# Moving the last rows' scores ahead of both value parts in an attention and mixture-of-experts kernel

## The chip, the cores and the metric

The kernel runs on one core of a Trainium2 chip. The time is device time in microseconds of one execution. The core has five engines, each with its own instruction stream: TensorE (PE; its weight loads are PEld), VectorE (DVE), ScalarE (ACT), GpSimd (POOL) and SyncE (SP, which issues most transfers).

## The reference

Three layers follow each other; the change lies in the first.

```python
# 1. attention: 4 batches, 8 heads, 576 positions, 64 columns per head
scores = scale * q @ k.T                       # per batch and head
cum = cumsum(maximum(s, 0)); bias = -(cum[:, None] - cum[None, :])
scores = where(causal, -1e9, scores + minimum(bias, 0))
attn = exp(scores - max(scores)); attn = attn / (sum(attn) + 1e-9)
x = (attn @ v) as (2304 tokens, 512)
# 2. mixture of experts: every token goes to the expert of its largest logit
logits = x @ w_gate; e = argmax(logits); gate = softmax(logits)[e]
x[tokens of e] = gate * (maximum(x[tokens of e] @ w1[e], 0) @ w2[e])    # 8 experts, 512 -> 1024 -> 512
# 3. three products and a maximum
h = maximum(maximum(x @ u1, x @ u2), x @ u3)                             # 512 -> 768
out = h @ w_out                                                          # 768 -> 512
```

## The kernel before, in words

The 32 heads are worked off as 16 pairs, and each pair p is spread over three periods. In period p its scores are formed and turned into exponentials; in period p+1 the exponentials are transposed and multiplied with the values; in period p+2 the result (oT) is turned back to rows, scaled by the sums and stored (`xrow`). So a period of the middle holds the scores of one pair, the transposes and value parts of the pair before, and the rows of the one before that. After the last period the expert layers follow, TensorE's matmuls nearly alone.

Every step is a Python function that is put into a heap with a place (`at(slot, fn)`), and at the end the functions are called in order of place (`run_events`). The order of calls is the order of instructions on each engine; the engines then run freely and wait for each other's data and buffers. A place is counted in slots of 0.456 us (`SLOT`) and a period is 25 slots (`IT`). The table `SEQ` (L93) gives the places of TensorE's steps in a period in microseconds; the steps that follow on other engines stand a number of slots later: `LR` (2.5) from scores to their reduction, `LE` (5.5) to the exponential, `LH` (1.5) from a transpose to its copy, `LV` (1.0) from a value part to its copy, `LN` (3.5) from the tail's exponential to its normalisation.

The steps of a period, by their names in `SEQ`:

- `s0` to `s7` are scores of the first 512 rows of both heads, in blocks of 128 rows (`scores`, L290): row block 3 (s0, s1, 512 columns), 1 (s2, s3), 2 (s4, s5, 384 columns) and 0 (s6, s7). TensorE writes two banks at s0, s2, s4 and s6 (L308). VectorE adds the bias and takes the minimum (`red`, L314) into one of three `ns` buffers, and ScalarE takes the exponential with its sum (`ex`, L321).
- `s8` and `s9` are the last rows, or the tail: the 64 rows from 512 of both heads in one block of 128, columns 0 to 255 and 256 to 575 (`tmm`, L328). Their reductions (`tred`, L335) write one buffer `nst`, one exponential follows (`tex`, L343), and `tnorm` divides by the sum (two small VectorE instructions, L348 and L349, and one of GpSimd, L350).
- `A0`, `B0`, `A1`, `B1`, `C2`, `C3` and `TT` are transposes of exponentials (`t_mm`, L376) into two banks in turn, copied into one buffer `ptT` (`t_ev`, L409): A1, B1 and TT by VectorE (L414), the others by ScalarE (L416). TT holds the tail's columns 0 to 511; its copy writes four strips of 64 columns per head, at 512, 960, 1408 and 1856 of `ptT`.
- `v0` and `v1` are the value parts (`v_mm`, L418): v0 makes output columns 0 to 255, from columns 0 to 255 and 576 to 703 of `ptT`, and v1 columns 256 to 575, from all key blocks and with the tail's strips in them. Each writes one of two banks that `xrow` uses too. `v_ev` (L430, L435) copies them to `oT`; at v0's copy GpSimd also clears the last columns of `oT`.
- `x0` and `x1` are the rows of the pair before the last (L459, L464).

Score banks ("a") are four, taken in turn; the tail takes one bank each for s8 and s9. The last pair has its own order (`LSEQ`, `lpos`). When a batch of heads is finished, `route` (L475) puts some thirty small VectorE instructions and two groups of small matmuls, at steps of 1.8 or 1.6 slots, into the next periods. Three expert weights are split in two parts during the attention, by ScalarE (`w_hi`, L192) and VectorE (`w_lo`, L685), at slots 80, 126 and 172.

Of the kernel before, what the change touches and what calls it, by code (L numbers as in the profile page):

```python
# [59 lines left out]
T0, T1, T2, T3, T4 = -56, -56, -53, -51, -43  # L60
F0, F1, F2, F3 = 7, 9, 11, 19
BCE = "VAVAA"
LR, LE, LH, LV, LX, LN = 2.5, 5.5, 1.5, 1.0, 1.5, 3.5
NSB, PPB = 3, 4
CSL = 22
MA, MB, MT = 8, 0.5, 0
# [24 lines left out]


SEQ = {"A0": 0, "B0": 0.45, "s0": 0.9, "s1": 0.9, "s2": 1.95, "s3": 1.95, "A1": 2.65, "B1": 3.0, "x0": 3.35, "x1": 4.15,  # L93
       "s4": 4.7, "s5": 4.7, "s6": 5.55, "s7": 5.55, "C2": 6.0, "C3": 6.45, "v0": 6.8, "TT": 7.65, "s8": 8.1, "s9": 8.55,
       "v1": 9.1}
TDVE = ("A1", "B1", "TT")

# [1 line left out]
def emit(nc, tc, qt, kt, v, s, wg, w1, w2, m64, out, dbg=None):  # L99
# [9 lines left out]
    def bank(tag, dt=F32):  # L109
        return ps.tile([P, 512], dt, tag=tag, name="ps_" + tag, bufs={"a": 4, "b": 2, "c": 2}[tag])  # L110
# [49 lines left out]
    for b in (0, B - 1):  # L160
        t = cp.tile([P, 5, NG], F32, name=f"gx{b}")
# [26 lines left out]
    NP = B * H // 2  # L188
# [13 lines left out]
    def at(slot, fn, *args):  # L202
        heapq.heappush(evq, (slot, next(seqno), fn, args))
# [61 lines left out]
    def masks(p, t0, t1, t2):  # L265

        def wide():
            t = st[p]["bl"][:, 0:2048].rearrange("p (x w) -> p x w", w=512)[:, :, 128:256]
            G.affine_select(t, t, pattern=[[0, 4], [-1, 128]], compare_op=ALU.is_ge, fill=BIG, base=0,
                            channel_multiplier=1)  # L270

        def narrow(g):
            t = st[p]["bl"][:, 1024 * g:1024 * g + 768].rearrange("p (x w) -> p x w", w=128)[:, 0:5:4]
            G.affine_select(t, t, pattern=[[0, 2], [-1, 128]], compare_op=ALU.is_ge, fill=BIG, base=0,
                            channel_multiplier=1)

        def tail():
            for g in range(2):
                t = st[p]["bl"][64 * g:64 * g + 64, BW - 64:BW]
                G.affine_select(t, t, pattern=[[-1, 64]], compare_op=ALU.is_ge, fill=BIG, base=0, channel_multiplier=1)  # L280

        at(t0, wide)
        for g in range(2):
            at(t1[g], narrow, g)
        at(t2, tail)
# [84 lines left out]
    def ptv(p, tslots, vslots):  # L370
        d = st[p]

        def tr(pt, c, i, g, k0):
            T.transpose(pt[:, c:c + 128], (d["P", "t"] if g == "t" else d["P", g, i])[:, k0:k0 + 128], idf)  # L374

        def t_mm(u):  # L376
            pt = d["pt", u] = bank("b")
            if u[0] in "AB":
                g, j = "AB".index(u[0]), int(u[1])
                for i in range(j, 4):  # L380
                    tr(pt, 128 * (i - j), i, g, 128 * j)
            elif u == "C2":
                for g in range(2):
                    for i in (2, 3):
                        tr(pt, 256 * g + 128 * (i - 2), i, g, 256)
            elif u == "C3":
                for g in range(2):
                    tr(pt, 128 * g, 3, g, 384)
                tr(pt, 256, 0, "t", 512)
            else:  # L390
                for j in range(4):
                    tr(pt, 128 * j, 0, "t", 128 * j)

        def regions(u):
            pt = d["pt", u]
            two = lambda ap: ap.rearrange("p (g w) -> p g w", g=2)
            if u[0] in "AB":
                g, j = "AB".index(u[0]), int(u[1])
                w = 512 - 128 * j
                return [(lambda t: t[:, g, POFF[j]:POFF[j] + w], pt[:, :w])]  # L400
            if u == "C2":
                return [(lambda t: t[:, :, POFF[2]:POFF[2] + 256], two(pt))]
            if u == "C3":
                return [(lambda t: t[:, :, POFF[3]:POFF[3] + 128], two(pt[:, 0:256])),
                        (lambda t: t[:, :, POFF[4]:POFF[4] + 64], two(pt[:, 256:384]))]
            return [(lambda t: t[:, :, 512:PTW].rearrange("p g (j w) -> p g j w", w=64)[:, :, 0::TS // 64],
                     pt.rearrange("p (j g w) -> p g j w", j=4, g=2))]

        def t_ev(u):  # L409
            if "pt" not in st[p]:  # L410
                d["pt"] = ab.tile([P, 2, PTW], F32, tag="ptT", name="ptT", bufs=1)
            for f, src in regions(u):
                if u in TDVE:
                    V.tensor_copy(f(d["pt"]), src)  # L414
                else:
                    A.activation(f(d["pt"]), src, AF.Copy)  # L416

        def v_mm(x):  # L418

            c0, c1 = ((0, 256), (256, 576))[x]  # L420
            po = d["po", x] = bank("c")
            js = [j for j in range(5) if 128 * j < c1]
            for j in js:
                qa = max(c0, 128 * j)
                for g in range(2):
                    T.matmul(po[64 * g:64 * g + 64, qa - c0:c1 - c0], d["v"][:, g, j],  # L426
                             d["pt"][:, g, POFF[j] + qa - 128 * j:POFF[j] + c1 - 128 * j],
                             start=(j == 0), stop=(j == js[-1]))

        def v_ev(x):  # L430
            c0, c1 = ((0, 256), (256, 576))[x]
            if x == 0:
                d["oT"] = ab.tile([P, 640], F32, tag="oT", name="oT", bufs=2)
                G.memset(d["oT"][:, S:640], 0.0)
            A.activation(d["oT"][:, c0:c1], d["po", x][:, :c1 - c0], AF.Copy)  # L435

        for u, t in tslots.items():
            at(t, t_mm, u)
            at(t + LH, t_ev, u)
        for x, t in vslots.items():  # L440
            at(t, v_mm, x)
            at(t + LV, v_ev, x)

    def xrow(p, slots):
        d = st[p]
# [140 lines left out]
    for p in range(NP):  # L586
        t = IT * p
        load(p, t - 2 * IT + LD0 if p else -60)

        last_wide = [max(t + pos[f"s{2 * ORD.index(i) + g}"] for i in (1, 3)) + LR for g in range(2)]  # L590
        first = [min(t + pos[f"s{2 * ORD.index(i) + g}"] for i in (0, 2)) for g in range(2)]
        masks(p, t - 4 if p == 0 else t + min(pos[f"s{x}"] for x in range(4)) - MA,
              [max(last_wide[g] + 0.1, first[g] - MB) for g in range(2)], t - MT)
        scores(p, [t + pos[f"s{i}"] for i in range(10)])
        o = t + IT
        units = ("A0", "A1", "B0", "B1", "C2", "C3", "TT")
        tpos = {u: o + pos[u] for u in units}
        vpos = {x: o + pos[f"v{x}"] for x in range(2)}
        xpos = [o + IT + pos["x0"], o + IT + pos["x1"]]
        lpos = {u: IT * NP + LS0 + LSP * i for i, u in enumerate(LSEQ.split())}  # L600
        if p == NP - 2:
            xpos = [lpos["y0"], lpos["y1"]]
        if p == NP - 1:
            tpos = {u: lpos[u] for u in units}
            vpos = {x: lpos[f"v{x}"] for x in range(2)}
            xpos = [lpos["x0"], lpos["x1"]]
            for x in range(2):
                vpos[x] = max([vpos[x]] + [tpos[u] + LH + 0.02 for u in units if x or u[0] in "AB"])
            xpos[0] = max(xpos[0], max(vpos.values()) + LV + 0.02)
            xpos[1] = max(xpos[1], xpos[0] + 0.5)  # L610
        ptv(p, tpos, vpos)
        end = xrow(p, xpos)
        if p == NP - 1 - H // 2:
            TR2 = end
# [30 lines left out]
    t = TE  # L645
    S0, SL = [], []
    for x, gs in enumerate(STEPS):
        if x == NEARLY:
            t = TM
# [6 lines left out]
    def pt(g, i):  # L656

        x, k = step[g]
        us = SL[x] / 8 * i + sum(cost[o] for o in STEPS[x][:k]) / 8 + (GAP12 if i >= 4 else 0)
        return S0[x] + us / SLOT  # L660
# [99 lines left out]
    for n in range(24):  # L760
        dst = w32 if n < 18 else wo32
        i, x = divmod(n if n < 18 else n - 18, 2)
# [233 lines left out]
    for x, gs in enumerate(STEPS):  # L996
# [7 lines left out]
        for g in gs:  # L1004
# [8 lines left out]
            for kk in range(4):  # L1013
                t = t0 + st_ * kk
# [5 lines left out]
            for f in range(8):  # L1020
                t = pt(g, f // 2) + (f % 2) * L / 16 / SLOT
# [5 lines left out]
            for d_ in range(4):  # L1027
                t = pt(g, 4 + d_)
# [210 lines left out]
```

## Time and profile before

| | us |
|---|---|
| median of 3 runs | 795.99 (795.22 to 797.65) |
| profiled execution | 794.54 |
| its span, from first to last instruction | 792.8 |
| PE busy | 758.3 (96%) |
| PEld busy | 681.6 (86%) |
| DVE busy | 437.1 (55%) |
| ACT busy | 335.2 (42%) |
| POOL busy | 109.4 (14%) |

The busy times are sums over all instructions of an engine, and the shares are averages over a stage of attention (to about 200 us) and the expert stages behind it. A timeline row gives the start in us, the duration, the engine, the line, the operation, what it writes and reads, and the count; in brackets stands the idle time of the engine before it and who ended it. A matmul of 32-bit data appears as several instructions.

### The profile page before, as it was taken

The page shows a single profiled execution, that of the slowest core. Times are in us where ns is not written, and L with a number is a line of the kernel's source. Part 1 is how long each engine was busy: PE and PEld are TensorE (multiplying, and loading weights), DVE is VectorE, ACT ScalarE, POOL GpSimd, SP SyncE. Part 2 cuts the span into 40 slices and gives each one's busy share as a digit, 9 for nine tenths or more (in the row PEclk, how much of TensorE's full clock was granted, in tenths as well). Part 3 has the DMA queues.
Part 4 walks back from the last instruction along what each step waited for, and adds up shares of the span by engine and source line. Part 5 has one row for each costly group of instructions (what it writes and reads, how often), then busy time and mean ns, then how long its engine had stood idle before and what let it go on. Part 6 is the DMA issues. An engine that isn't in the chain of part 4 may idle for free. (4 is left out here: it accounts for less than half of the span.)

```text
span 792.8 us, 12891 instructions
## 1 busy us (share of the span) xinstructions
PE 758.3 (96%) x4782; PEld 681.6 (86%) x4782; DVE 437.1 (55%) x1142; ACT 335.2 (42%) x771; POOL 109.4 (14%) x226
## 2 busy tenths in 40 slices
PE   6999899999889999999999999999999999999996
PEld 4666666666789998999999999989999899898995
DVE  5667757678668686899888756412312223122120
ACT  5666666666546343555455544221121212212111
POOL 3332332333030200101200000010010000100001
PEclk9999999999999999999999999999999999999999
DMA  5887858767386687868776535000010000100001
GB/s 154 238 216 217 212 160 225 194 181 222 135 281 210 221 310 256 308 221 281 238 230 214 204 97 172 26 31 10 1 41 1 26 14 1 41 1 14 26 1 41
DMA packets 34876, 112.43 MB, mean 142 GB/s; under 512 B 4793, under 2 KB 4875, under 8 KB 32891
## 3 DMA queue, kind: packets, MB, share of 16 engines
q1 hardware_dynamic: 24107, 81.66, 34.6%
q10 hardware_dynamic: 7456, 18.89, 6.7%
q0 software_dynamic: 3248, 11.03, 4.1%
q8 instruction: 39, 0.64, 0.3%
q14 instruction: 26, 0.21, 0.1%
HBM read 94.97 MB, written 16.60 MB: 141 GB/s over the span
## 5 line engine op out<-in xcount | busy, mean ns | idle before, releaser
L1135 DVE TENSOR_TENSOR mA<-ps_a,mA 128x384 f32<-128x384 f32 x72 | 40.2, 558 | 181.4 <-PE ps_a L942 181.4
L942 PE MATMUL ps_a<-yc,wq 128*128 128x384 f32 x720 | 129.1, 339 | 0.0
L942 PEld LDWEIGHTS ps_a<-yc,wq 128*128 128x128 f32 x720 | 127.4, 188 | 0.4
L942 PE MATMUL ps_c<-h,wq 128*128 128x336 f32 (+1 forms) x672 | 106.2, 316 | 3.1 <-ACT yT L988 1.6
L942 PEld LDWEIGHTS ps_c<-h,wq 128*128 128x128 f32 x672 | 101.8, 192 | 3.8 <-ACT yT L988 2.0
L942 PE MATMUL ps_a<-yc,wm 128*128 128x384 f32 x576 | 103.7, 339 | 0.0
L942 PE MATMUL ps_a<-xT,wq 128*128 128x336 f32 (+1 forms) x648 | 101.0, 313 | 1.1 <-DVE h L967 1.1
L942 PEld LDWEIGHTS ps_a<-yc,wm 128*128 128x128 f32 x576 | 101.9, 188 | 0.0
L942 PEld LDWEIGHTS ps_a<-xT,wq 128*128 128x128 f32 x648 | 96.5, 188 | 1.7 <-DVE h L967 1.4
L321 ACT ACTIVATE P<-ns,mn 128x512 f32<-128x512 f32 (+3 forms) x128 | 70.6, 558 | 14.9 <-DVE mn L314 14.7
L942 PE MATMUL ps_c<-wm,g 128*128 128x512 f32 x324 | 76.9, 396 | 0.0
L1139 ACT ACTIVATE g<-mA 128x384 fp32r<-128x384 f32 x36 | 18.9, 526 | 135.7 <-DVE mA L1135 135.7
L942 PEld LDWEIGHTS ps_c<-wm,g 128*128 128x128 f32 x324 | 60.9, 188 | 14.4
L1158 POOL DMA_INDIRECT out<-o,midi x18 | 17.5, 973 | 378.1 <-ACT o L1154 373.9
L314 DVE CUSTOM_DVE_ANT_0 ns<-ps_a,bl 128x512 f32<-128x512 f32 (+3 forms) x128 | 57.5, 488 | 19.5 <-PE ps_a L308 8.1
L685 DVE TENSOR_TENSOR wq<-wr,wq 128x1024 fp32r<-128x1024 f32 x44 | 53.9, 1226 | 10.4 <-ACT wq L192 9.7
L426 PEld LDWEIGHTS ps_c<-ptT,nv 128*64 128x64 f32 x448 | 29.8, 138 | 31.5 <-DVE ptT L414 13.3
L426 PE MATMUL ps_c<-ptT,nv 128*64 128x320 f32 (+4 forms) x448 | 51.4, 367 | 5.4 <-DVE ptT L414 5.2
L192 ACT ACTIVATE wq<-wr 128x1024 fp32r<-128x1024 f32 x44 | 46.3, 1056 | 17.9 <-DMA wr<-in_w 17.9
L308 PE MATMUL ps_a<-nk,nq 64*128 64x512 f32 (+3 forms) x256 | 47.0, 472 | 3.4 <-DVE mn L314 1.8
L374 PE MATMUL ps_b<-idf,P 128*128 128x128 f32 x320 | 47.1, 284 | 2.0 <-DVE ptT L414 1.2
L963 ACT ACTIVATE h<-ps_a 128x336 fp32r<-128x336 f32 (+1 forms) x64 | 28.0, 440 | 46.0 <-PE ps_a L942 45.4
(221 smaller groups left out, 953.5 us busy)
## 6 DMA issues: line engine op xcount, KB each, us to landing
wr<-in_w SPq DMA_DIRECT2D x49, 512.0 KB, 4.8
bl<-cumd SPq DMA_DIRECT2D x30, 528.0 KB, 9.1
dr<-in_m ACTq DMA_DIRECT2D x24, 512.0 KB, 4.5
xr<-in_w SPq DMA_DIRECT2D x23, 512.0 KB, 4.8
nq<-in_qt SPq DMA_DIRECT2D x16, 352.0 KB, 3.7
nv<-in_v SPq DMA_DIRECT2D x16, 320.0 KB, 9.5
nk<-in_kt SPq DMA_DIRECT2D x16, 288.0 KB, 2.9
xd<-xr SPq DMA_DIRECT2D x4, 1152.0 KB, 6.5
```

Source lines behind the costliest of these rows:

```text
L192: A.activation(o, x, AF.Copy)
L308: T.matmul(d["sp", i, g][:, :w], d["q"][r, 128 * i:128 * i + 128], d["k"][r, :w], start=True, stop=True)
L314: V.tensor_tensor_reduce(out=ns[:, :w], in0=d.pop(("sp", i, g))[:, :w], in1=d["bl"][:, 1024 * g + BOFF[i]:1024 * g + BOFF[i] + w], scale=- ...
L321: A.activation(pp, d.pop(("ns", i, g))[:, :w], AF.Exp, bias=d["mn"][:, c:c + 1], scale=-1.0, accum_out=ssum[b][:, i, h + g:h + g + 1])
L374: T.transpose(pt[:, c:c + 128], (d["P", "t"] if g == "t" else d["P", g, i])[:, k0:k0 + 128], idf)
L426: T.matmul(po[64 * g:64 * g + 64, qa - c0:c1 - c0], d["v"][:, g, j], d["pt"][:, g, POFF[j] + qa - 128 * j:POFF[j] + c1 - 128 * j], start=( ...
L685: (V if eng == "V" else G).tensor_tensor(t[:, 1], raws.pop(key), t[:, 0].bitcast(F32), ALU.subtract)
L942: T.matmul(ps_, w_(zw), x_(zx), start=(first and n == 0), stop=(last and n == 2))
L963: A.activation(t[:, 0, :c], hT[n, f, "p"][:, :c], AF.Relu)
L1135: V.tensor_tensor(m, pm[:, :CH], m, ALU.max)
L1139: A.activation(t[:, 0], h2[c, f, "m"], AF.Copy)
L1158: G.indirect_dma_start(out, bass.IndirectOffsetOnAxis(ap=midi[:, n:n + 1].bitcast(U32), axis=0), h2.pop((c, x, "s")), None)
```

## The change

Three edits. In `SEQ` the tail's scores s8 and s9 come at 6.8 and 7.25, TT at 7.75, v0 at 8.3 and v1 at 9.1 as before; the order of these steps on TensorE becomes s8, s9, TT, v0, v1 in place of v0, TT, s8, s9, v1. `LV` becomes a pair of delays: v0's copy stays 1.0 slots behind v0, and v1's copy is put 4.5 slots behind v1. The last pair keeps 1.0 for both.

```diff
-LR, LE, LH, LV, LX, LN = 2.5, 5.5, 1.5, 1.0, 1.5, 3.5
+LR, LE, LH, LV, LX, LN = 2.5, 5.5, 1.5, (1.0, 4.5), 1.5, 3.5
...
-       "s4": 4.7, "s5": 4.7, "s6": 5.55, "s7": 5.55, "C2": 6.0, "C3": 6.45, "v0": 6.8, "TT": 7.65, "s8": 8.1, "s9": 8.55,
+       "s4": 4.7, "s5": 4.7, "s6": 5.55, "s7": 5.55, "C2": 6.0, "C3": 6.45, "s8": 6.8, "s9": 7.25, "TT": 7.75, "v0": 8.3,
        "v1": 9.1}
...
             at(t, v_mm, x)
-            at(t + LV, v_ev, x)
+            at(t + (LV[0] if p == NP - 1 else LV[x]), v_ev, x)
...
-            xpos[0] = max(xpos[0], max(vpos.values()) + LV + 0.02)
+            xpos[0] = max(xpos[0], max(vpos.values()) + LV[0] + 0.02)
```

## Rows read from the trace of the kernel before

**Rows 1.** Windows: us, busy time (instructions) of each engine, PEclk, DMA share, GB/s

```profile
104.27:115.41 11.14, 11.14 (x86) 7.77 (x84) 7.35 (x29) 7.93 (x25) 3.73 (x8) 1.00 0.68 177
...
345.00:385.00 40.00, 40.00 (x270) 39.93 (x269) 34.71 (x74) 20.34 (x36) 2.81 (x3) 1.00 0.76 244
```

**Rows 2.** Waits of PE between 30 and 205 us: total, times, longest

```profile
PE ps_c L426 <- DVE ptT L414: 3.4, 8, 1.1
```

**Rows 3.** Timeline of PE: A0 and B0 at the head of two periods

```profile
64.54 1.09 PE L374 MATMUL ps_b<-idf,P 128*128 128x128 f32 x8
...
90.54 1.09 PE L374 MATMUL ps_b<-idf,P 128*128 128x128 f32 x8
```

**Rows 4.** Timeline of PE: one undisturbed period, A0 to the next A0

```profile
104.26 1.09 PE L374 MATMUL ps_b<-idf,P 128*128 128x128 f32 x8
105.28 1.56 PE L308 MATMUL ps_a<-nk,nq 64*128 64x512 f32 x8
...
109.87 0.88 PE L374 MATMUL ps_b<-idf,P 128*128 128x128 f32 x6
...
110.79 0.87 PE L426 MATMUL ps_c<-ptT,nv 128*64 128x256 f32 x8
111.59 0.66 PE L374 MATMUL ps_b<-idf,Pt 128*128 128x128 f32 x4
112.08 1.14 PE L328 MATMUL ps_a<-nk,nq 128*128 128x256 f32 x4
113.19 2.27 PE L426 MATMUL ps_c<-ptT,nv 128*64 128x320 f32 x20
115.40 1.09 PE L374 MATMUL ps_b<-idf,P 128*128 128x128 f32 x8
```

**Rows 5.** Timeline of DVE in the same period

```profile
106.54 0.69 DVE L314 CUSTOM_DVE_ANT_0 ns<-ps_a,bl 128x512 f32<-128x512 f32 x1 [0.59 <-PE ps_a L308]
...
110.55 0.55 DVE L314 CUSTOM_DVE_ANT_0 ns<-ps_a,bl 128x384 f32<-128x384 f32 x1
...
111.03 0.56 DVE L314 CUSTOM_DVE_ANT_0 ns<-ps_a,bl 128x384 f32<-128x384 f32 x1
...
112.23 0.29 DVE L314 CUSTOM_DVE_ANT_0 ns<-ps_a,bl 128x128 f32<-128x128 f32 x1 [0.43 <-ACT P L321]
...
112.45 0.69 DVE L414 COPY ptT<-ps_b 128x512 f32<-128x512 f32 x1
113.05 0.41 DVE L335 CUSTOM_DVE_ANT_0 nst<-ps_a,bl 128x256 f32<-128x256 f32 x1
...
113.62 0.55 DVE L335 CUSTOM_DVE_ANT_0 nst<-ps_a,bl,mn 128x320 f32<-128x320 f32 x1
114.10 0.08 DVE L335 DVE_READ_ACCUMULATOR2_ANT mn<- 128x1 f32 x1
```

**Rows 6.** Timeline of ACT at the start of the next period

```profile
115.85 0.77 ACT L343 ACTIVATE Pt<-nst,mn 128x576 f32<-128x576 f32 x1
...
116.61 1.07 ACT L416 ACTIVATE ptT<-ps_b 128x512 f32<-128x512 f32 x2
```

**Rows 7.** Timeline of ACT and DVE in the fifth and seventh period

```profile
65.75 1.04 ACT L192 ACTIVATE wq<-wr 128x1024 fp32r<-128x1024 f32 x1
...
68.17 0.68 DVE L314 CUSTOM_DVE_ANT_0 ns<-ps_a,bl 128x512 f32<-128x512 f32 x1
...
90.99 1.05 ACT L192 ACTIVATE wq<-wr 128x1024 fp32r<-128x1024 f32 x1
...
92.07 1.23 DVE L685 TENSOR_TENSOR wq<-wr,wq 128x1024 fp32r<-128x1024 f32 x1 [1.81 <-ACT wq L192]
...
94.03 0.69 DVE L314 CUSTOM_DVE_ANT_0 ns<-ps_a,bl 128x512 f32<-128x512 f32 x1
```

**Rows 8.** Timeline of DVE: TT's copy in period 1, a routing instruction

```profile
27.18 0.69 DVE L414 COPY ptT<-ps_b 128x512 f32<-128x512 f32 x1 [0.68 <-PE ps_b L374]
...
74.33 0.45 DVE L494 TENSOR_TENSOR r_L<-r_L,r_L 128x40 f32<-128x40 f32 x1
```

## Prediction

> **What bounds the kernel now.** The windows come first, because the share of busy time over the whole span mixes two stages [rows 1]. Up to about 200 us the kernel does the attention, one pair of heads per period; after that come the two expert stages. In the stretch 345 to 385 TensorE is busy for all of its 40.00 us: the later stages are TensorE's own work, so that what the attention loses at its end arrives at the end of the kernel. The period from 104.27 is 11.14 us long and TensorE is busy for 11.14 of them, VectorE for 7.35, ScalarE for 7.93. Periods with nothing else among their instructions have this length; those with a weight rounding or the routing of a finished batch are longer. The second view is TensorE's waits: from 30 to 205 us it lost 3.4 us, in 8 gaps, ahead of a value part that waited for a copy of VectorE into ptT [rows 2]. That is all the time that the wait in question holds.
>
> The third view is the timeline of one undisturbed period on three engines. I give times from the start of A0 (104.26 us). TensorE [rows 4]: C2 and C3 from 5.61, v0 from 6.53 (0.80 to the next start), TT from 7.33 (0.49), s8 and s9 from 7.82 (1.11), v1 from 8.93 (2.21), next A0 at 11.14. Nothing is idle between them. VectorE [rows 5]: the reduction of s0 starts at 2.28, after 0.59 us of waiting for TensorE; from there it works without a break (s4 6.29 to 6.84, s5 6.77 to 7.33) up to the reduction of s7, which waits 0.43 us for an exponential on ScalarE and starts at 7.97. At 8.19 follows TT's copy, which ends at 8.88, and v1 starts at 8.93. So v1, which reads TT's columns with its first matmul, starts 0.05 us after that copy: the copy has no slack at all, although VectorE is idle for a third of the period.
>
> **The change part by part.** No instruction is added or removed; only places in the queues change. The places below are those of the code, in its microseconds (SEQ plus a delay; a delay is a number of slots of 0.456).
>
> *TensorE.* New order: C2, C3, s8, s9, TT, v0, v1. s8 takes the score bank that s4 used (four banks, and s4 is four allocations back), and has to wait for the reduction of s4. TensorE gets there at 6.53, the reduction ends at 6.84; with the 0.05 us that v1 shows after its releaser s8 starts at 6.89, a stall of 0.36 us. s9 needs the reduction of s5 (7.33), when s8 has just been issued: nothing more. s8 and s9 end at 8.00, TT at 8.49, v0 at 9.29 [rows 4, 5].
>
> *VectorE.* It goes through its list in order. Places before: reductions of s6 and s7 at 6.69, TT's copy at 8.33, reductions of s8 and s9 at 9.24 and 9.69. After: 6.69; s8 at 7.94, s9 at 8.39, TT's copy at 8.43. Both tail reductions now stand ahead of TT's copy. s7's reduction still starts at 7.97, for its wait hangs on C2's and C3's copies and the exponential of s4, which are not moved. s8's starts at 8.19 (its scores are there since about 7.5), s9's 0.57 us later at 8.76, as in the rows, and the next instruction 0.48 us after that, at 9.24. TT's copy then runs from 9.24 to 9.93, and v1 starts at 9.98 instead of 8.93: **1.05 us later**. TensorE's own order would have allowed 9.29, so the bank stall of 0.36 is inside this time and not on top of it. The next period's A0, s0 and with them the first reduction follow v1, so nothing in the next period recovers it: the loop is 12.19 us. Bounds for one period: 0.36 us if the copy came in time and only the bank bound; 1.14 if the reductions cost 0.57 each with nothing overlapped. I take 1.05, which comes from start-to-start times of these very instructions.
>
> On the bank the Trainium skill has a rule (Perfetto Trace Analysis, Optimization Strategy): one gap repeating on the engine that should be saturated can mean that there are too few buffers for the next tile. By that rule the new gap would be s8's 0.36 us and the remedy another bank; by the rows the copy is later than the bank, and the sum by the rule alone is the second rival below.
>
> *ScalarE.* v0's copy moves from 7.26 to 8.76, behind the exponentials of s6 and s7; the tail's exponential moves from 11.06 to 9.76, and v1's copy from 9.56 to 11.15, behind it. Before, the exponential and A0's copy stood behind v1's copy; from 115.85 to 116.61 the exponential alone held A0's and B0's copies up by 0.76 us [rows 6]. In an undisturbed period that frees nothing for TensorE, which had no gap there. It does in two periods with a weight rounding. In the seventh (A0 at 90.54 [rows 3]) the rounding at 90.99 stood behind v1's copy; VectorE's subtraction at 92.07 waited for it, and the first reduction started at 94.03 where 92.82 (2.28 after A0) was possible [rows 7]. The rounding (slot 172) now comes ahead of v1's copy (174.5) and fills ScalarE's idle time: 1.21 us back. In the fifth (A0 at 64.54) the first reduction started at 68.17 where 66.82 was possible; the rounding at 65.75 moves up by the exponential's 0.76: 0.76 us back.
>
> *GpSimd and SyncE.* The two memsets and the tail's normalisation move with the copies and the exponential. oT's memset now stands behind the wide mask and may wait there for the mask's load, but its columns are read only 4 us into the next period. The tail's mask comes behind the normalisation and is needed after 8 us of the next period: cost nothing, cover several us. No DMA is moved; SyncE's loads of the next q and k are freed earlier with s9.
>
> *Sum, against the profiled execution (794.54 us; its span is 792.8).* Sixteen pairs; the last has an order of its own, so 15 periods hold the moved steps. The first runs cold: TT's copy waited 0.68 us for TensorE there [rows 8], starting 0.75 after VectorE was free, and v1 started 0.18 after the copy; of 1.05 some 0.1 remains. Fourteen others: 14.7. Less 1.21 and 0.76. In the six periods with routing, small instructions stand among the reductions and partly wait for each other, as the one at 74.33, which took 0.45 us for 40 columns [rows 8]; the two reductions take up some of that, about 1 us in all (an estimate from this row). 0.1 + 14.7 - 1.97 - 1.0 = 11.8 us, so 806.4 us. The median of the runs shown is 795.99, 1.45 us above the profiled run: **808 us**.
>
> **The rivals.**
>
> *ScalarE sets the front of the period (faster).* With the exponential gone from ahead of A0's copy, the first reduction starts up to 0.76 us earlier. Then s4's reduction ends at 6.08 (no bank stall), TT's copy at 9.17, and v1 goes at 9.29 or before as TensorE allows; the 3.4 us of gaps and the 1.97 us go: 789.2, or 790.6 beside the runs. It decides at one point: whether the first reduction is released by ScalarE. The fifth and seventh periods speak for it [rows 7], against it the 0.59 us wait for TensorE in the undisturbed period, and s7's wait, which hangs on C3's copy and not on the first reduction [rows 5]. 6%. A rule of the Trainium skill says the same by another way (Perfetto Trace Analysis, Identifying the Most-Contended Engine): for VectorE occupancy tells its load, and the engine to work on is the fullest. By it VectorE, at 66% of the period, has room for two early reductions, and this rival's time would come out; the trace differs, as the copy ends 0.05 us ahead of its reader in spite of the 66%.
>
> *Only the bank binds (no change).* If TT's copy is in time for some other reason, 15 times 0.36 us come, and 3.4 and 1.97 go: 794.6, beside the runs 796. For it: the stall is certain in order. Against it: VectorE's list. 3%.
>
> *v0 waits for TT's copy too (slower still).* TT's copy writes four strips of columns between 512 and 1920 of ptT; v0 reads 0 to 255 and 576 to 703, which lie between the strips. If the wait were drawn around all strips together, v0's 0.80 us would also come after the copy: 15 times 0.8 more, 820. Nothing in the rows shows it either way, as v0 stood ahead of TT; exact strips are likelier. 5%.
>
> **How the numbers follow.** Forecast 86%, the rivals 6, 3 and 5. A measurement of this kernel can tell about 0.3% from no change, 2.4 us. Faster 0.06, no change 0.04, slower 0.90. Of the forecast's own range, 1.14 us in all 15 periods less the 1.97, and a little beyond the shading, gives 811 to 813; 0.7 us in thirteen periods and 4 us back gives 801. I take 801 to 814, which leaves out the three rivals (14 in 100) and the ends of the forecast.
>
> **What would show it.** Right: in an undisturbed period A0 to A0 takes about 12.2 us; v1 waits about 0.7 us for VectorE's copy into ptT, in nearly every period; s8 waits about 0.35 us for a reduction; TT's copy starts right behind the second tail reduction; the tail's exponential stands ahead of v1's copy; the seventh period is no longer than before. Wrong: periods still of 11.1 us, or v0 waiting for the copy. If the first reduction starts less than 2.2 us after A0, the first rival is at work.

## Result and profile after

The changed kernel takes 807.3 us (median of 6 runs, 806.59 to 809.67) against 796.61 for the kernel before (6 runs, 794.50 to 798.03): the ratio is 1.014 with a 95% interval of 1.0119 to 1.0161. It is slower, by 10.7 us; 808 was forecast. The profiled execution took 806.91 us with a span of 805.2, 12.4 us more than the span before; the profiled execution before, 794.54 us, lies 2.1 us under the median of its kernel, so the profiles differ by more than the medians.

The difference lies in the attention alone. From the start of the last period, A0 at 198.88 us before and 211.36 after, to the end of the span it is 593.9 us before and 593.8 after. First the waits of TensorE between 30 and 220 us in the kernel after (total us, times, longest):

```profile
PE ps_c L426 <- DVE ptT L414: 12.1, 15, 1.6
PE ps_a L328 <- DVE mn L314: 4.9, 10, 1.0
```

The first line was 3.4 us in 8 waits up to 205 us [rows 2], ahead of the last pair's value parts. Of the 15 waits now, one of 1.3 us is the last pair's, which the kernel before has too; the other 10.8 us are 14 waits, one in each period from the second to the fifteenth. The first period, which ends at 31.24, has one too (0.90 us, below). The second line, the tail's scores waiting for a bank, is new. One undisturbed period shows both, as it did before [rows 4]. This is TensorE's timeline of the kernel after, A0 to the next A0:

```profile
108.80 1.09 PE L374 MATMUL ps_b<-idf,P 128*128 128x128 f32 x8
...
114.41 0.88 PE L374 MATMUL ps_b<-idf,P 128*128 128x128 f32 x6
...
115.71 1.28 PE L328 MATMUL ps_a<-nk,nq 128*128 128x256 f32 x4 [0.31 <-DVE mn L314]
116.83 0.60 PE L374 MATMUL ps_b<-idf,Pt 128*128 128x128 f32 x4
117.36 0.87 PE L426 MATMUL ps_c<-ptT,nv 128*64 128x256 f32 x8
118.78 2.28 PE L426 MATMUL ps_c<-ptT,nv 128*64 128x320 f32 x20 [0.55 <-DVE ptT L414]
120.98 1.09 PE L374 MATMUL ps_b<-idf,P 128*128 128x128 f32 x8
```

And VectorE's in the same period, beside [rows 5]:

```profile
115.10 0.55 DVE L314 CUSTOM_DVE_ANT_0 ns<-ps_a,bl 128x384 f32<-128x384 f32 x1
...
116.77 0.29 DVE L314 CUSTOM_DVE_ANT_0 ns<-ps_a,bl 128x128 f32<-128x128 f32 x1 [0.43 <-ACT P L321]
...
116.99 0.42 DVE L335 CUSTOM_DVE_ANT_0 nst<-ps_a,bl 128x256 f32<-128x256 f32 x1
...
117.56 0.55 DVE L335 CUSTOM_DVE_ANT_0 nst<-ps_a,bl,mn 128x320 f32<-128x320 f32 x1
...
118.04 0.69 DVE L414 COPY ptT<-ps_b 128x512 f32<-128x512 f32 x1
```

Counted from A0 (108.80), s7's reduction still starts at 7.97 us and still waits 0.43; the two tail reductions come next; TT's copy starts at 9.24 instead of 8.19, and v1 at 9.98 instead of 8.93. The period is 12.18 us in place of 11.14. The window says it once more (us, busy time of PE, PEld, DVE, ACT, POOL, granted clock, DMA share, GB/s):

```profile
108.80:120.98 12.18, 11.32 (x87) 7.80 (x83) 7.35 (x29) 8.15 (x25) 3.35 (x9) 1.00 0.69 173
```

VectorE does the same 7.35 us of work [rows 1]; only their order has changed. The granted clock stays at 1.00, TensorE's upper level of 2.4 GHz.

What the change gave back stands in the seventh period (A0 at 95.45), in ScalarE's and VectorE's timeline of the kernel after:

```profile
92.68 0.77 ACT L343 ACTIVATE Pt<-nst,mn 128x576 f32<-128x576 f32 x1 [0.33 <-DVE mn L335]
...
93.45 1.04 ACT L192 ACTIVATE wq<-wr 128x1024 fp32r<-128x1024 f32 x1
...
94.53 1.23 DVE L685 TENSOR_TENSOR wq<-wr,wq 128x1024 fp32r<-128x1024 f32 x1
...
95.56 0.44 ACT L435 ACTIVATE oT<-ps_c 128x320 f32<-128x320 f32 x1 [1.07 <-PE ps_c L426]
...
97.73 0.69 DVE L314 CUSTOM_DVE_ANT_0 ns<-ps_a,bl 128x512 f32<-128x512 f32 x1 [1.21 <-PE ps_a L308]
```

The exponential and the weight rounding now run before v1's copy, while v1 is still being computed. The first reduction starts 2.28 us after A0 and waits for TensorE, where before it started 3.49 us after A0, behind the weight's subtraction [rows 3, 7].

### The profile page after: what moved, and what is told of

Read it like the earlier page. It is cut to its first block, busy times and chain, and to the rows that moved or that the text cites. A ratio compares the mean times of both kernels' runs of the same rounds, so it can differ in the third digit from the quotient of the medians.

```text
span 805.2 us, 12895 instructions
## 1 busy us (share of the span) xinstructions
PE 757.9 (94%) x4782; PEld 680.8 (85%) x4782; DVE 438.3 (54%) x1142; ACT 338.2 (42%) x771; POOL 110.3 (14%) x226
## 5 line engine op out<-in xcount | busy, mean ns | idle before, releaser
L685 DVE TENSOR_TENSOR wq<-wr,wq 128x1024 fp32r<-128x1024 f32 x44 | 53.6, 1221 | 10.8 <-ACT wq L192 10.2
L915 POOL DMA_INDIRECT xw<-xd,gi x22 | 24.4, 1108 | 167.0 <-PE ps_b L921 111.0
```

The costliest lines, as they stand in the source:

```text
L685: (V if eng == "V" else G).tensor_tensor(t[:, 1], raws.pop(key), t[:, 0].bitcast(F32), ALU.subtract)
L915: G.indirect_dma_start(xw[n][x][0:k], None, rows, bass.IndirectOffsetOnAxis(ap=src[0:k, c:c + 1].bitcast(U32), axis=0))
```

## Experiments

The theory: v1's start hangs on the place of TT's copy in VectorE's list, and the third edit (v1's copy behind the exponential) is a separate gain in the two periods with a weight rounding. The rivals: the bank that s8 waits for is what costs; ScalarE sets the front of every period. Beside the times I give the stretch from the second A0 to the sixteenth, read from each trace: 14 periods, without the first, whose length also goes with the granted clock (last section). It is 168.63 us in the kernel before (30.25 to 198.88) and 180.12 in the changed one (31.24 to 211.36).

**v0 back in front of s8** (edit against the changed kernel; v0's copy keeps its place, and the last pair its delays):

```diff
-LR, LE, LH, LV, LX, LN = 2.5, 5.5, 1.5, (1.0, 4.5), 1.5, 3.5
+LR, LE, LH, LV, LX, LN = 2.5, 5.5, 1.5, (4.4, 4.5), 1.5, 3.5
...
-       "s4": 4.7, "s5": 4.7, "s6": 5.55, "s7": 5.55, "C2": 6.0, "C3": 6.45, "s8": 6.8, "s9": 7.25, "TT": 7.75, "v0": 8.3,
+       "s4": 4.7, "s5": 4.7, "s6": 5.55, "s7": 5.55, "C2": 6.0, "C3": 6.45, "v0": 6.75, "s8": 6.8, "s9": 7.25, "TT": 7.75,
```

> The changed kernel with v0 put back behind C3 (order C2, C3, v0, s8, s9, TT, v1; all copies and reductions in the changed order). s8 then comes to TensorE 0.8 us later and finds its bank free. List theory (v1 waits for TT's copy, which stands behind two reductions): the bank wait was hidden, periods stay at 12.2 us, the time is that of the changed kernel within 1 us (about 807). Bank theory (s8's wait for s4's reduction is what costs): 0.36 us less in 15 periods, 5.4 us faster than the changed kernel.

Measured: 807.0 us, ratio to before 1.0138 (1.0116 to 1.016); the stretch 179.98 us. One undisturbed period of it on TensorE:

```profile
107.44 1.09 PE L374 MATMUL ps_b<-idf,P 128*128 128x128 f32 x8
...
113.96 0.87 PE L426 MATMUL ps_c<-ptT,nv 128*64 128x256 f32 x8
114.76 1.24 PE L328 MATMUL ps_a<-nk,nq 128*128 128x256 f32 x4
115.84 0.60 PE L374 MATMUL ps_b<-idf,Pt 128*128 128x128 f32 x4
117.41 2.28 PE L426 MATMUL ps_c<-ptT,nv 128*64 128x320 f32 x20 [0.97 <-DVE ptT L414]
119.62 1.09 PE L374 MATMUL ps_b<-idf,P 128*128 128x128 f32 x8
```

s8 waits for nothing any more (its bank waits fall from 4.9 us to 0.2), and v1 still starts 9.97 us after A0. What was a bank wait is now a longer wait for the copy: 0.97 instead of 0.31 and 0.55. The bank was hidden, as forecast, and it is not the cause.

**TT's copy alone, moved in the kernel before:**

```diff
-       "v1": 9.1}
+       "v1": 9.8}
...
-            at(t + LH, t_ev, u)
+            at(t + (4.6 if u == "TT" and p < NP - 1 else LH), t_ev, u)
```

> The kernel before with one thing moved: TT's copy on VectorE comes behind the two tail reductions (v1's place is moved with it, with nothing passed over, so that TensorE's order stays v0, TT, s8, s9, v1). List theory: s8's and s9's scores come to VectorE at about 8.5 and 9.1 us of the period, the copy ends at about 10.3 and v1 starts there instead of at 8.93: periods of 12.5 us, 18 to 21 us slower than before. Bank theory: TensorE's order is the old one and s8 waits for no bank, so no change.

Measured: 814.94 us, ratio 1.0236 (1.0214 to 1.0258), 19.6 us over the kernel before in the same comparison; undisturbed periods 12.46 us. TensorE's order is the old one. On VectorE the copy stands behind the reductions until 120.17, and TensorE waits for it:

```profile
119.12 0.42 DVE L335 CUSTOM_DVE_ANT_0 nst<-ps_a,bl 128x256 f32<-128x256 f32 x1 [0.19 <-PE ps_a L328]
...
119.69 0.55 DVE L335 CUSTOM_DVE_ANT_0 nst<-ps_a,bl,mn 128x320 f32<-128x320 f32 x1
...
120.17 0.68 DVE L414 COPY ptT<-ps_b 128x512 f32<-128x512 f32 x1
...
120.91 2.27 PE L426 MATMUL ps_c<-ptT,nv 128*64 128x320 f32 x20 [1.29 <-DVE ptT L414]
```

So the order on VectorE costs by itself, and more here, since the tail's scores come later in the old order.

**TT's copy ahead of the tail's reductions, in the changed kernel:**

```diff
-            at(t + LH, t_ev, u)
+            at(t + (0.3 if u == "TT" and p < NP - 1 else LH), t_ev, u)
```

> The changed kernel with TT's copy put ahead of the two tail reductions on VectorE; TensorE's and ScalarE's order stay changed. List theory: the copy waits only for TT's transposes (done at 8.6 us of the period), runs from about 8.8 to 9.5, v1 starts at about 9.55 instead of 9.98, periods of 11.75 us: some 6 us faster than the changed kernel, some 6 us slower than the kernel before. Bank theory: as the changed kernel, within 1 us.

Measured: 797.15 us, ratio 1.0019 (1.0003 to 1.0035), 1.8 us over the kernel before; the stretch 169.63 us. The direction is the theory's, but the size was missed: I had expected 6 us over the kernel before. The copy came a little earlier (8.66 to 9.35 us after A0), so that it no longer bound: v1 follows v0 without a wait, and undisturbed periods are 11.61 us, not 11.75. What is left of the 0.47 us over 11.14 is s8's bank (0.30 us of waiting in the trace) and slightly longer steps behind it; so the bank does cost once the copy is not late. The periods with routing also came back by more than the undisturbed ones: the sixth by 1.45 us against the changed kernel (14.14 to 12.69), the tenth by 1.26. Against the kernel before, the third edit, which is in this version, hides part of the loss: the fifth period takes 12.00 us against 13.10, the seventh 12.42 against 13.72.

**Four buffers ns, in the changed kernel:**

```diff
-NSB, PPB = 3, 4
+NSB, PPB = 4, 4
```

> The changed kernel with four buffers ns in place of three. s7's reduction then finds a free buffer and doesn't wait for the exponential of s4 (0.43 us in undisturbed periods, 1.38 in the sixth and tenth, 0.85 in the seventh and eleventh). List theory: what counts is when VectorE reaches TT's copy, so all of this comes back, down to where TT's transposes or TensorE's own order bind: undisturbed periods of about 11.75 us, 7 to 9 us faster than the changed kernel. Bank theory: s8's bank waits for s4's reduction, which does not move: as the changed kernel, within 1 us.

Measured: 799.62 us, ratio 1.0049 (1.0032 to 1.0066); the stretch 172.45 us, 7.7 less than in the changed kernel. In an undisturbed period (A0 at 103.23) the reduction of s7 follows that of s6 without a wait, and everything behind it moves forward:

```profile
110.45 0.29 DVE L314 CUSTOM_DVE_ANT_0 ns<-ps_a,bl 128x128 f32<-128x128 f32 x1
...
110.66 0.29 DVE L314 CUSTOM_DVE_ANT_0 ns<-ps_a,bl 128x128 f32<-128x128 f32 x1
...
110.87 0.42 DVE L335 CUSTOM_DVE_ANT_0 nst<-ps_a,bl 128x256 f32<-128x256 f32 x1
...
111.45 0.55 DVE L335 CUSTOM_DVE_ANT_0 nst<-ps_a,bl,mn 128x320 f32<-128x320 f32 x1
...
111.76 3.18 PE L426 MATMUL ps_c<-ptT,nv 128*64 128x256 f32 x28
...
111.92 0.69 DVE L414 COPY ptT<-ps_b 128x512 f32<-128x512 f32 x1
```

The copy ends at 9.38 us after A0, v0 and v1 run through, and the period is 11.64 us (103.23 to 114.87). A buffer that has nothing to do with the tail took out most of the loss, because the wait for it stood ahead of the copy in the same list. The bank wait is still there (4.7 us in 10 waits).

**The third edit alone, in the kernel before:**

```diff
-LR, LE, LH, LV, LX, LN = 2.5, 5.5, 1.5, 1.0, 1.5, 3.5
+LR, LE, LH, LV, LX, LN = 2.5, 5.5, 1.5, (1.0, 4.5), 1.5, 3.5
...
-            at(t + LV, v_ev, x)
+            at(t + (LV[0] if p == NP - 1 else LV[x]), v_ev, x)
```

> The kernel before with the third edit alone: v1's copy goes behind the tail's exponential, the order on TensorE and VectorE stays. Theory (only TT's copy and a late first reduction reach TensorE): undisturbed periods stay at 11.14 us, the fifth and the seventh give back about 0.95 and 1.2 us, so the whole is about 2.2 us (0.27%) faster than before. Rival (ScalarE sets the front of every period): 0.4 to 0.7 us less in each of 15 periods, 6 to 10 us faster. Rival (the delay of v1's copy costs): slower by a bank wait at x1, up to 0.3 us per period, 4 us.

Measured: 793.02 us against 795.32, ratio 0.9975 (0.9956 to 0.9995); the stretch 166.25 us, 2.4 less than before. Undisturbed periods stay at 11.13 us; the fifth is 11.90 (13.10 before), the seventh 12.50 (13.72). So ScalarE does not set the front of every period; the gain is 1.2 us in each of the fifth and the seventh period, where the first reduction stood behind a rounding. The third period holds a rounding too and gains 0.1 us.

**The third edit undone, in the changed kernel:**

```diff
-            at(t + (LV[0] if p == NP - 1 else LV[x]), v_ev, x)
+            at(t + LV[0], v_ev, x)
```

> The changed kernel with the third edit undone: v1's copy 1.0 slots behind v1 again, ahead of the tail's exponential. Theory: undisturbed periods stay at 12.18 us, the fifth and the seventh lose about 0.95 and 1.2 us again: 2.2 us slower than the changed kernel (about 1.7% slower than before). Rival (the third edit gives nothing, or costs): as the changed kernel, or faster.

Measured: 812.85 us, ratio 1.0225 (1.019 to 1.026); the stretch 183.56 us, 3.4 more than in the changed kernel, of which the fifth period holds 0.9 and the seventh 1.8. The medians lie 5.5 us apart, each from its own comparison; the profiled execution, 810.11 us, is the fastest of the four. The direction is as expected and the size larger: in the seventh period the routing's matmul then waits 2.2 us, up to a first reduction that stands behind the late rounding on VectorE.

**Two versions to beat both.** The kernel before with the third edit and four buffers ns, and the same with TT's copy nearer to its transposes (the second of these edits):

```diff
-NSB, PPB = 3, 4
+NSB, PPB = 4, 4
...
-            at(t + LH, t_ev, u)
+            at(t + (0.2 if u == "TT" and p < NP - 1 else LH), t_ev, u)
```

> A version to beat both: the kernel before with the third edit and four buffers ns. Undisturbed periods stay at 11.14, TensorE's own work; the sixth, seventh, tenth and eleventh lose their 0.27 us ahead of v1, so about 1.1 us faster than the third edit alone, 3.3 us (0.4%) faster than before. If VectorE's order were no limit in the old order, as the third edit alone.

> The version above, and TT's copy 0.2 instead of 1.5 slots behind its transposes, so that in the periods with routing it stands ahead of one more small VectorE instruction. In the fifth, ninth and thirteenth period v1's wait (1.1, 0.57 and 0.56 us) falls by 0.1 to 0.4 us each: another 0.5 to 1 us faster, about 4 us (0.5%) faster than before. If the copy waited for its transposes there and held up the instructions behind it: no faster than the version above.

Measured: 790.35 us, ratio 0.9936 (0.9913 to 0.9958), stretch 163.73 us, for the first; 788.88 us, ratio 0.9915 (0.989 to 0.994), stretch 162.98, for the second, against 796.06 of the kernel before. Each gained rather more than expected: the first 2.5 us in the stretch over the third edit alone (1.1 expected), with undisturbed periods of 11.09 us, where v1 starts as soon as TensorE is there. The second version is faster than the first by 0.75 us in the stretch; between their intervals the runs can't tell them apart. Both beat the kernel before and the changed one. TensorE's waits between 30 and 225 us in the second:

```profile
PE ps_c L426 <- DVE ptT L414: 2.2, 3, 1.3
PE ps_a L308 <- DVE r_rv L517: 1.6, 2, 0.8
```

Of the waits for VectorE's copies into ptT, 5.2 us in the same window before, 2.2 are left, 1.8 of them in the last pair.

## Why the prediction was right

- **TT's copy behind two reductions, 1.05 us per period: right.** The undisturbed periods are 12.18 and 12.19 us. The times in the period came out to a few hundredths: s8 at 6.91 (6.89 forecast), the copy at 9.24 (9.24), v1 at 9.98 (9.98). v1's wait is 0.55 us, where about 0.7 was forecast, for TensorE came to it a little later than the sum had it. The sum from start-to-start times of rows of the same instructions holds because nothing but their order was changed. Moving the copy alone in the old order showed that the order by itself is enough.
- **The bank wait is inside it: right,** shown by v0 in front of s8, where it went and the time stayed. With TT's copy early it binds, and the period is 11.61 us. By a rule of the Trainium skill (Perfetto Trace Analysis, Optimization Strategy), a gap that repeats on the engine that should be saturated can mean too few buffers. Here taking the bank wait away changed nothing (807.0 us), and the buffer that did help (ns, 799.62 us) belonged to a wait of VectorE.
- **The third edit gives back 1.21 and 0.76 us: right in place, too small in size.** In the seventh period the first reduction moved from 3.49 to 2.28 us behind A0, as forecast. In the fifth it moved from 3.63 to 2.68, 0.95 in place of 0.76. By length, the edit alone made these periods 1.22 and 1.20 us shorter; in the changed kernel the two together became 0.74 us shorter, where the sum has them 0.13 longer.
- **The first period, 0.1 us: wrong.** It became 0.95 us longer, and the cause is the same as in the others. This is v1 of the first period in the kernel before and in the kernel after:

```profile
28.05 2.27 PE L426 MATMUL ps_c<-ptT,nv 128*64 128x320 f32 x20
```

```profile
29.04 2.27 PE L426 MATMUL ps_c<-ptT,nv 128*64 128x320 f32 x20 [0.90 <-DVE ptT L414]
```

  Before, the copy waited for TensorE [rows 8], and I took that slack as still there. In the changed kernel VectorE starts s7's reduction at 27.03, goes on with the two tail reductions and starts the copy at 28.30; TensorE is done with v0 by then, and v1 waits. The last section compares this period in more runs.
- **About 1 us for the reductions filling small gaps of the routing: too large.** VectorE has routing instructions in nine periods, not six (5 to 7, 9 to 11 and 13 to 15). In the seven of them that are neither the fifth nor the seventh, the growth falls short of 1.05 us by 0.25 us in all. The term was an estimate, and no run separates it.
- **The sum, 11.8 us against 12.4 between the profiled spans: right by mechanism, close in part by luck.** The first period and the routing together came out some 1.6 us longer than the sum has them, the fifth and the seventh period 0.9 us shorter. Between the medians the difference is 10.7 us (9.5 to 12.8 by the interval), where the forecast, 808 against 795.99, has 12.0. That 807.3 lies so near to 808 is also because the median before came out at 796.61.
- **Nothing recovers it later: right.** From the last A0 on, the two executions differ by 0.1 us.
- **v0 does not wait for TT's copy:** it starts 0.53 us after TT's first transpose, ahead of the copy, in the timeline after. The rival in which ScalarE sets the front fell with the third edit alone. By a rule of the Trainium skill (Perfetto Trace Analysis, Identifying the Most-Contended Engine), occupancy tells VectorE's load. The way to the rival's time by that rule fell too: VectorE is busy for 7.35 of 12.18 us in the period after, 60%, and it is the one that TensorE waits for.

## What to carry to other kernels

An engine that is idle for a third of a period can still set its length: read what stands ahead of the one instruction that the busy engine waits for, in the list of the engine that does it. Moving work earlier in such a list moves all behind it later, and the price can be read from start-to-start times of the rows before the change is made. Look for the waits that stand ahead in the same list: a fourth buffer for another step was worth 7.7 us in the changed kernel. And try the parts of a change alone; one of three edits was a gain that the other two hid.

## What the runs showed of the hardware

The first period is 12.3 to 15.5 us long in the ten profiles. Two things go with its length: the granted clock, and whether v1 waits for TT's copy. These are windows of the same stretch in the third edit alone, the kernel after, and the kernel before with the third edit and four buffers ns, whose first periods took 12.34, 14.94 and 15.53 us:

```profile
16.00:30.00 14.00, 12.98 (x85) 8.85 (x85) 8.07 (x37) 9.88 (x32) 4.46 (x11) 1.00 1.02 288
```

```profile
16.00:30.00 14.00, 10.81 (x61) 7.59 (x63) 8.01 (x35) 9.00 (x30) 4.23 (x9) 0.88 1.01 284
```

```profile
16.00:30.00 14.00, 11.80 (x57) 8.05 (x59) 6.81 (x30) 8.09 (x27) 4.54 (x11) 0.76 0.90 246
```

The number behind the five busy times is the granted clock: 1.00, 0.88 and 0.76 as means over the stretch, between the two levels of 1.2 and 2.4 GHz. The kernel before has 0.88 and 13.99 us in it: the clock is 1.00 up to 22 us, 0.80 from 22 to 24, 0.50 (the lower level) from 24 to 26, 0.84 from 26 to 28 and 1.00 again behind that. Before it fell, TensorE had waited 0.45 us ahead of the matmul at 14.30, 0.66 ahead of that at 16.26 and 1.83 ahead of that at 21.45. In the third edit alone, with the same order on TensorE, there is only the last of these waits, 1.02 us long, and the clock stays at 1.00. But with v0 in front of s8 TensorE waited 0.65 and 1.92 us at the second and the third of these places, and the clock stayed at 1.00 too. So what sets it from run to run stays open.

At the same mean clock the copy makes the difference. With 1.00 the first period takes 12.34 us (third edit alone) and 12.68 (four buffers ns in the changed kernel), where v1 does not wait; it takes 13.60 (third edit undone), 13.65 (v0 in front of s8) and 13.85 (TT's copy alone), where v1 waits 0.91, 0.95 and 1.29 us for TT's copy. With 0.88 it takes 13.99, 14.04 and 14.12 us without that wait and 14.94 in the changed kernel, with 0.90 us of it. From the matmul of s4 to the next A0 it is 7.31 us in the third edit alone and 8.36 with v0 in front of s8, both at 1.00: the 1.05 us of the other periods. Because the clock has its part in the first period, the stretch from the second A0 on was compared.
